# A fused attention and FFN kernel on one core: last denominators by a broadcast-sum matmul, b2 and b1 as matmul rows, and another table of the work's split

## The chip, the core and the metric

The kernel runs on one core of a Trainium2 chip. The core has a matrix engine (TensorE, PE in the profile), VectorE (DVE), ScalarE (ACT), GpSimd (POOL) and SyncE (SP), which issues transfers. The metric is the device time of one execution, in microseconds; before the change it is 747.16 us, the median of three runs (747.12 to 747.19).

## The reference

The input is a sequence of 2048 rows of 512. It is normalised, and the normalised rows go through two branches whose results are added to the input: attention with 32 query heads of 16 and a single shared key and value head, and a feed-forward layer of width 1792 with biases.

```python
xn = _layernorm(x, axis=-1)
return x + _A_ref(xn, A_wq, A_wk, A_wv, A_wo) + _B_ref(xn, B_w1, B_b1, B_w2, B_b2)
...
scores = jnp.einsum("bhqd,bkd->bhqk", q, k) * (Dh ** -0.5)
p = _softmax(scores, axis=-1)
o = jnp.einsum("bhqk,bkd->bhqd", p, v) 
...
h = _gelu(jnp.einsum("bsd,df->bsf", x, w1) + b1) 
return jnp.einsum("bsf,fd->bsd", h, w2) + b2
```

The attention result goes through `wo`, and the GELU is the tanh form. Most of the work is the softmax: 32 heads x 2048 x 2048 exponentials, 134 million.

## The kernel before

**Tiles.** The sequence is cut into four blocks of 512 query columns, and the heads into eight groups of four. For each block and group (32 head groups in all) the 16 key tiles of 128 are gone through for the four heads, so there are 2048 score tiles of 128 keys x 512 queries. Three tiles make a unit, and 683 units make the main part. `scores(u)` forms three tiles with three matmuls that run side by side on 32 rows of the array each (L968), into one half of six PSUM banks; the halves alternate.

**Who exponentiates what.** Each tile is done by one of two engines. ScalarE takes it with its exponential (`exp`, L991): two tiles of a unit in one instruction of 1024 columns, or three in one of 1536. Or VectorE takes it: one `tensor_scalar` adds a constant to the scores and writes them as int16 (L1022, `p1`), which are then read as bf16; the exponential's error is evened out by adding four shifted copies of the same tile. The shifts are made in batches of up to six tiles by three steps (`close_batch`): two on VectorE on the whole batch and on two copies at once (L1069), and one per tile that goes to GpSimd if it is free at that moment and to VectorE otherwise (L1065). A tile of ScalarE needs one matmul with V on PE, a tile of VectorE five (L1035). These use one of four column groups of 32, one for each head, and add up in bank 6. V carries a column of ones, so row 16 of each head's 32 rows is the softmax denominator. The string `DTAB` says for each unit which of its tiles VectorE takes; it is a constant of the file.

**Order.** Nothing is ordered by hand beyond that. All operations are recorded with their dependencies, a planner (`Prog.schedule`) goes through them with its own costs and puts each engine's instructions into one fixed order, and semaphores are placed. Side work (the products of the FFN, the query projections, the output projection) is placed behind units given by tables: `HP` for the first FFN product of each tile, `YP` for the output tiles, `QK` and `Q3` for queries. Fillers (matmuls with zeros) are put where the planner sees PE idle.

**FFN and GELU.** The first FFN product of a tile of 128 features x 512 rows (`h_mm`, four products of four column groups each, L674) goes into bank 7, and VectorE adds b1 from `b1T` and writes bf16 (L1177). The GELU is not taken there: it needs another table of ScalarE, so all GELUs are collected in two blocks, after units 182 and 512 (`GU`, function `gelu`). A block loads the table, and takes for two query blocks: seven tiles from SBUF in one instruction, three single tiles from PSUM, seven from SBUF, three from PSUM, five from SBUF, three from PSUM. The tiles from PSUM (`h_late`) were never evacuated by VectorE: their products stand in three banks of one half, ScalarE reads them with b1 as a bias operand (L1202), and the bank that it frees takes the product of the tile three places later. During a block the scores use one half of the banks, and VectorE takes all of the exponentials of the four or five units concerned. The table for the exponential is loaded again by the compiler ahead of the next exponential.

**Output.** When a head group ends, its 128 x 512 sums are copied to SBUF (`o_evac`, L1081). The denominators go by DMA into a dense form, are inverted by VectorE, go to memory and come back broadcast over 16 rows each, and GpSimd or VectorE multiplies (L1112) into `oTp`, two head groups to 128 rows. The output projection of a row tile (`wo_mm`) adds four such products, `y_mm` the second FFN product, `b2_mm` the bias as a product of ones and a row, all into bank 7.

**The tail.** The last head group takes no transfers. `o_norm_last` copies its sums in two halves (L1120), picks the denominators out with fp32 matmuls that bring them to 128 rows x 4 (`selL`, L668), inverts these on VectorE (L1126), spreads each over 32 columns (half of it on VectorE, L1132, half on ScalarE, L1134), transposes back on PE (L1137) and multiplies from PSUM (L1141). Then come the last projection (`wol`), three additions on VectorE (L1356), one copy on ScalarE (L1359) and four stores. The second-last head group shares no 128 rows with it: its 64 rows of `oTp` have zeros beneath them.

Of the kernel before, what the change touches and what calls it, by code (L numbers as in the profile page):

```python
# [60 lines left out]
DTAB = "o2t00o20.20.t0t.2.o2oot..0t0oo.o.2o2t2o220.200.t00tt.2.0o222o.002.020ttt0..t202ot.2.22222o.o002.t200o.0t..2002t22.2o.o2220t.t2o.2ooo02to..20t0o000.0.to00o0ot.2.22t2.0t0oo.0oo02t..020bXxxto0o0.tt220tot00.ot020t.t0tt..200t02t.t02o.2o202.2222t202.ot0000.2o.2.t0t2t0t0t2.00222o2o..t.2t02.22t02o.t2200o..222.o0.t.000o02o2.2o..ttoo.o.too0oo0.0t.22.2t22o.o0oo..2ot0.ooo.totot.22tt20o..2toto.02ott0t0.tt02oo.o00..to00to0t0..00t2o..t22o0to2002o.2tt2.022t.2.0ot00o0020o0t.20.ooo.t..00o0..t2o2o22o..t20.ootot0t0t02220t00.0bbXXB2t2o20t2.2o202t..t02t0..o2o2oo22t20o..200to20ot022..tt02t0.2.22o202t20too..202oot.ot20000ot0..2oto0.0t.2ot02o2020t.ot.022o2o..000o0t.to2o.2t0.0o.to2t0t0.o0.oto2.2t.o.."  # L61
# [14 lines left out]
HP = ((46.3963,25.57262,48.16392,137.89013,14,52.2867,77,21.34724,36.94639,135.1619,35.25214,143.76585,89,72.22155),(112.2259,74.41715,95,121.29838,157.97442,0,0,0,0,0,0,0,0,0),(328.87654,322.51607,297.61552,309.7649,294.71218,291.30051,286,332.83416,338.02598,344.7955,303.57085,313.20872,350.63119,488.80201),(479.44121,503.08827,457.33229,508.56788,448.62794,0,0,0,0,0,0,0,0,0))  # L76
YP = ((186.87977,183,230.37357,220.85148),(347,407.00376,373.24541,414.87978),(521,545,576.59107,557),(600,612.80493,650.61865,662))
# [460 lines left out]
def bass_parallel_sum__grouped_kv_mqa__dense_activation_gelu__prompt_kernel(  # L538
# [33 lines left out]
    with ExitStack() as es:  # L572
# [20 lines left out]
        b1row = sb([FT, P], bf, "b1row")  # L593
# [9 lines left out]
        selL = sb([P, 4], f32, "selL")  # L603
        rT = sb([P, 4, 4], f32, "rT")
# [32 lines left out]
        rX = rbP[:, 0, :].rearrange("p (i r) -> p i r", i=4)  # L637
# [54 lines left out]
        dma("sp", b1row[:], B_b1.rearrange("(k p) -> k p", p=P), "d_b1", w=["b1row"], due=0.6, lat=9.0)  # L692
# [43 lines left out]
        for gl in range(2):  # L736
# [3 lines left out]
        tload = act(lambda e: e.add_instruction(mybir.InstLoadActFuncSet(name=nc.get_next_instruction_name(), engine=e.engine,  # L740
                                                                         ins=[], outs=[], act_func_set_id=LNEXP_SET)),
# [337 lines left out]
        def o_evac(gg):  # L1079
# [23 lines left out]
            if end:  # L1103
                dve(lambda e: e.memset(oTp[64:P, sl, :], 0.0), r=[("Of", i)], w=[("oTp", sl)], n=200, lock=True)
# [300 lines left out]
```

## Time and profile before

| | |
|---|---|
| median of three runs | 747.16 us |
| the profiled execution, its own time | 747.11 us |
| its span, first to last instruction | 745.3 us |
| busy: PE, DVE, ACT, POOL | 729.3, 730.7, 730.1, 380.7 us |
| exponentials on ACT (L991) | 678 instructions, 676.9 us busy |
| score reads on DVE (L1022) | 552 instructions, 374.9 us busy |
| first GELU block | 209.26 to 225.56 us |
| second GELU block | 551.73 to 568.03 us |
| granted clock of TensorE | 1.000 |

The page gives busy time for each engine, a chain of work followed back from the last instruction, and groups of instructions by line with the mean duration of one. Instructions of one engine overlap a little, so that a mean duration is longer than the distance between two starts. PE's matmuls are pipelined, and its busy share says little of how near it is to its peak. The 1.81 us between the span and the execution's own time lie around the instructions.

### The profile page before, as it was taken

What the parts mean: (1) busy time and instruction counts of PE and PEld (TensorE: products, weight loads), DVE (VectorE), ACT (ScalarE), POOL (GpSimd) and SP (SyncE); (2) the same over time, 40 slices, a digit from 0 to 9 for tenths busy, and PEclk for the clock granted to TensorE, in tenths of its full rate; (3) what the DMA queues carried; (4) which work ended last, traced back from release to release, by engine and by line L of the source; (5) the groups of instructions that cost most, each with busy time, mean ns of one, the idle gap of its engine ahead of it and who ended that gap; (6) DMA issues with size and microseconds to landing.
All of it is one profiled execution on the core that took longest, in us unless ns stands there. A gap on an engine that the chain in (4) does not pass through costs nothing.

```text
span 745.3 us, 21947 instructions
## 1 busy us (share of the span) xinstructions
PE 729.3 (98%) x9050; PEld 222.9 (30%) x9050; DVE 730.7 (98%) x1402; ACT 730.1 (98%) x760; POOL 380.7 (51%) x528
## 2 busy tenths in 40 slices
PE   7999999999999999999999999999999999999998
PEld 5332322222232332223222222222233222322223
DVE  7899999999999999999999999999999999999996
ACT  8999999999999999999999999999999999999995
POOL 5445453566635465544636555454444555456361
PEclk9999999999999999999999999999999999999999
DMA  9200100101010010000101010100100001010010
GB/s 310 68 16 16 25 16 14 28 9 19 9 43 18 17 44 18 23 25 13 35 5 28 25 38 17 30 22 15 26 13 23 22 20 45 17 36 27 11 35 32
DMA packets 32076, 23.33 MB, mean 31 GB/s; under 512 B 16369, under 2 KB 27498, under 8 KB 31978
## 3 DMA queue, kind: packets, MB, share of 16 engines
q1 hardware_dynamic: 30922, 21.90, 11.0%
q8 instruction: 72, 1.18, 0.7%
q14 instruction: 26, 0.21, 0.1%
q10 hardware_dynamic: 1056, 0.03, 0.1%
HBM read 13.08 MB, written 2.35 MB: 21 GB/s over the span
## 4 chain that ended last, share of the span: by engine, by line
ACT 75%; PE 21%; DVE 3%; DMA 1%; issue 0%; SPq 0%
ACT E L991 70%; PE pAll L1035 10%; PE pAll L968 7%; PE pAll L674 4%; ACT ub L1198 2%; ACT x_sb L1202 1%; DVE Dt L1022 1%; PE pAll L668 1%; DVE stats L761 1%; ACT x_sb L1198 1%; DMA x_sb<-in_A_x_dram 1%; DVE Dt L1069 0%; ACT L991 0%; ACT L1198 0%; PE pAll L812 0%; ACT xnT L817 0%
## 5 line engine op out<-in xcount | busy, mean ns | idle before, releaser
L991 ACT ACTIVATE E<-pAll 128x1024 bf16<-128x1024 f32 (+1 forms) x678 | 676.9, 1242 | 2.1 <-PE pAll L968 2.0
L1065 POOL TENSOR_SCALAR Dt<-Dt 128x512 int16<-128x512 int16 x444 | 340.3, 766 | 326.8 <-DVE Dt L1069 136.3
L1035 PE MATMUL pAll<-Dt,V 128*32 128x512 bf16 x2825 | 422.4, 383 | 0.2
L1022 DVE TENSOR_SCALAR Dt<-pAll 128x512 int16<-128x512 f32 (+1 forms) x552 | 374.9, 693 | 2.8 <-PE pAll L968 2.1
L1069 DVE TENSOR_SCALAR Dt<-Dt 128x1024 int16<-128x1024 int16 (+6 forms) x518 | 290.8, 585 | 0.2
L968 PE MATMUL pAll<-QT,KT 32*128 32x512 bf16 x2048 | 267.2, 385 | 6.6 <-ACT E L991 4.1
L1035 PE MATMUL pAll<-E,V 128*32 128x512 bf16 x1483 | 272.1, 384 | 0.1
L968 PEld LDWEIGHTS pAll<-QT,KT 32*128 32x128 bf16 x2048 | 66.6, 91 | 288.4 <-ACT E L991 274.0
L1035 PEld LDWEIGHTS pAll<-Dt,V 128*32 128x32 bf16 x2825 | 108.8, 94 | 115.3 <-issue 76.8
L674 PE MATMUL pAll<-xnT,w_sb 128*32 128x512 bf16 x896 | 111.3, 382 | 0.9 <-ACT x_sb L1202 0.9
L1035 PEld LDWEIGHTS pAll<-E,V 128*32 128x32 bf16 x1483 | 64.6, 94 | 47.1 <-issue 31.9
L674 PE MATMUL pAll<-w_sb,ub 128*32 128x512 bf16 x448 | 70.0, 383 | 0.0
L674 PE MATMUL pAll<-w_sb,x_sb 128*32 128x512 bf16 x448 | 69.2, 383 | 0.0
L674 PE MATMUL pAll<-wop,oTp 128*32 128x512 bf16 x256 | 46.1, 383 | 0.0
L674 PEld LDWEIGHTS pAll<-xnT,w_sb 128*32 128x32 bf16 x896 | 31.2, 95 | 22.6 <-issue 9.5
L1065 DVE TENSOR_SCALAR Dt<-Dt 128x512 int16<-128x512 int16 x121 | 32.0, 282 | 0.0
L1112 POOL TENSOR_TENSOR oTp<-OfP,rbP 128x256 bf16<-128x256 f32 (+1 forms) x29 | 23.9, 831 | 13.7 <-DVE Dt L1069 9.2
L674 PE MATMUL pAll<-xnT,wq_sb 128*32 128x512 bf16 x256 | 24.3, 384 | 0.0
L1081 DVE COPY Of<-pAll 128x512 f32<-128x512 f32 x31 | 21.0, 679 | 0.0
L1177 DVE TENSOR_SCALAR ub<-pAll,b1T 128x512 bf16<-128x512 f32 x28 | 20.7, 739 | 0.0
L674 PEld LDWEIGHTS pAll<-w_sb,ub 128*32 128x32 bf16 x448 | 17.4, 94 | 5.5 <-issue 3.4
L674 PEld LDWEIGHTS pAll<-w_sb,x_sb 128*32 128x32 bf16 x448 | 16.6, 95 | 6.9 <-issue 5.2
(123 smaller groups left out, 251.7 us busy)
## 6 DMA issues: line engine op xcount, KB each, us to landing
OfP<-Of SPq DMA_DIRECT2D x124, 32.0 KB, 1.9
rbP<-rden_rows SPq DMA_DIRECT2D x124, 32.0 KB, 1.8
w_sb<-in_B_w_dram SPq DMA_DIRECT2D x2, 1792.0 KB, 12.7
x_sb<-in_A_x_dram SPq DMA_DIRECT2D x8, 256.0 KB, 4.6
x_sb<-in_A_x_dram SPq DMA_DIRECT2D x16, 128.0 KB, 2.1
QT<-qp SPq DMA_DIRECT2D x124, 16.0 KB, 1.8
out_dram<-x_sb SPq DMA_DIRECT2D x12, 128.0 KB, 1.7
wq_sb<-in_A_wq_dram SPq DMA_DIRECT2D x1, 512.0 KB, 6.4
```

Source lines behind the costliest of these rows:

```text
L668: return add("pe", lambda e: e.matmul(o, l, rh, start=start, stop=stop, **kw), r, w, occ=occ, lat=dlat[1], allow=allow, **ak)
L674: add("pe", lambda e, c=c, j=j: e.matmul(o[c, :], l[:, c], rh, start=start, stop=stop, tile_position=(0, 32 * j)), r, [(k, j) for k in w] ...
L968: ins = e.matmul(o, l, rh, start=True, stop=True, tile_position=(q0, 0))
L991: o = act(lambda e: e.activation(E[:, s0:s0 + na, :], bank(b0, na).rearrange("p (a n) -> p a n", a=na), ACT.Exp, scale=LN2 / 128.0), w=[B( ...
L1022: op = dve(lambda e: e.tensor_scalar(Dt[:, s:s + n, :], bank(bk, n).rearrange("p (a n) -> p a n", a=n), float(127 * 128) + SPL_D, SPL_MIN, ...
L1035: add("pe", lambda e, a, b: e.matmul(pO[32 * j:32 * j + 32, :], V1[:, v, kt, :], rhs, start=a, stop=b, tile_position=(0, 32 * j)), r=r + [ ...
L1065: add("pool", lambda e, d=d, k=k: e.tensor_scalar(d, d, 1.0, float(k), ALU.mult, ALU.add), [], [(("D", base[o > 0] + q), o)], occ=PL_OCC, ...
L1069: dve(lambda e, d=view(o, nb), q=view(i, nb), k=k: e.tensor_scalar(d, q, float(k), None, ALU.add), r=keys(i), w=keys(o), n=nb * n * TBW, m ...
L1081: dve(lambda e: e.tensor_copy(Of[:, i, :], pO), w=["O", ("Of", i)], allow=0.0)
L1112: "pool", lambda e, c=c: e.tensor_tensor(oTp[0:n, sl, c], OfP[0:n, s, c], rbP[0:n, s, c], ALU.mult),
L1177: dve(lambda e: e.tensor_scalar(ubs[tb % 2][:, ft, :], pM, b1T[:, ft:ft + 1], None, ALU.add), r=["b1T"], w=M4 + [ukey(tb, ft)], n=TBW + 57 ...
L1198: o = act(lambda e, uu=uu: e.activation(uu, uu, ACT.Gelu_apprx_tanh), r=uk, w=uk, n=len(uk) * TBW + 1200 * load + 50, kind="gelu", due=0.0 ...
```

## The change

Four things change, and with them the constants of the plan.

1. **Last denominators.** `selL` (128 x 4) becomes `selB` (128 x 128), in which every column of a head's 32 has a one at that head's denominator row. One fp32 matmul for each half of 256 columns gives the denominators already spread over the rows. ScalarE takes the logarithm of that from PSUM and then the exponential of its negative, in place of VectorE's reciprocal; the copies and transposes go. VectorE multiplies from SBUF.
2. **Last b2.** The 64 unused rows of `oTp` in the second-last group are set to 1 instead of 0, and their output weights are a new tile `wopE`, with 64 rows of `wo`, b2 in row 64, and zeros. For the last four row tiles `b2_mm` goes.
3. **FFN bias of the PSUM tiles as a matmul row.** `h_late` starts with a product of `b1row` (now 128 rows, zero past the 14) and one column of the identity, broadcast over 512 columns. ScalarE then needs no bias, and the first three PSUM tiles of each block are taken by one instruction of 1536 columns. The load of the table for the exponential is issued right behind the last GELU, and names the same set as the load at the start of the kernel. b1's transfer moves from the start of the kernel to behind the setup of K.
4. **The table.** `DTAB`, `HP`, `YP` have other values. Counted from the string, VectorE takes 568 tiles instead of 565.

In the order that results, ACT has 546 exponentials of two tiles and 128 of three (543 and 131 before), PE 72 bias matmuls more, 16 b2 matmuls less and 20 fillers more, POOL 453 of the one-tile steps (444 before).

The new constants of the plan (`DTAB`, `HP`, `YP`) are left out here.

```diff
-GU = tuple((u, tbs, n, (("s", tbs[0], 0, 7), ("p", tbs[1], 5), ("p", tbs[1], 6), ("p", tbs[1], 7), ("s", tbs[0], 7, 7), ("p", tbs[1], 8),
-                         ("p", tbs[1], 9), ("p", tbs[1], 10), ("s", tbs[1], 0, 5), ("p", tbs[1], 11), ("p", tbs[1], 12), ("p", tbs[1], 13)))
+GU = tuple((u, tbs, n, (("s", tbs[0], 0, 7), ("p", tbs[1], 5, 3), ("s", tbs[0], 7, 7), ("p", tbs[1], 8, 1), ("p", tbs[1], 9, 1),
+                         ("p", tbs[1], 10, 1), ("s", tbs[1], 0, 5), ("p", tbs[1], 11, 1), ("p", tbs[1], 12, 1), ("p", tbs[1], 13, 1)))
            for u, tbs, n in ((182, (0, 1), 5), (512, (2, 3), 5)))
+G_LOAD = (1.588, 1.405)
...
-        setup(lambda e: e.tensor_copy(selL[:], ident[:, 16:113:32]), r=["ident"], w=["selL"], due=24.0, after=late)
+        setup(lambda e: e.tensor_copy(selB[:].rearrange("p (j r) -> p j r", j=4), ident[:, 16:113:32].unsqueeze(2).to_broadcast([P, 4, 32])),
+              r=["ident"], w=["selB"], occ=0.3, due=24.0, after=late)
+        setup(lambda e: e.memset(wopE[:], 0.0), w=["wopE"], occ=0.4, due=24.0, after=late)
+        dma("sp", wopE[0:64, :], A_wo[(H - 2 * HG) * Dh:(H - HG) * Dh, :], "d_we", w=["wopE"])
+        dma("sp", wopE[64:65, :], B_b2.rearrange("(o n) -> o n", o=1), "d_we", w=["wopE"])
+        setup(lambda e: e.memset(b1row[:], 0.0), w=["b1row"], occ=0.16, due=24.0, after=late)
+        dma("sp", b1row[0:FT, :], B_b1.rearrange("(k p) -> k p", p=P), "d_b1", w=["b1row"])
...
-                dve(lambda e: e.memset(oTp[64:P, sl, :], 0.0), r=[("Of", i)], w=[("oTp", sl)], n=200, lock=True)
+                dve(lambda e: e.memset(oTp[64:P, sl, :], 1.0), r=[("Of", i)], w=[("oTp", sl)], n=200, lock=True)
...
         def o_norm_last(gg):
-            RB1 = [[("rbP", 0, h, j) for j in range(HG)] for h in range(2)]
             for h in range(2):
                 c = slice(h * 256, h * 256 + 256)
                 dve(lambda e, c=c: e.tensor_copy(Of[:, 1, c], pO[:, c]), w=["O", ("Of", 1), ("Of", 2 + h)], n=256, due=0.0)
             for h in range(2):
-                for i in (2 * h, 2 * h + 1):
-                    mm(bank(h)[:, 4 * i:4 * i + 4], Of[:, 1, i * P:(i + 1) * P], selL[:], True, True,
-                       r=[("Of", 2 + h), "selL"], w=[B(h)], occ=0.2, due=0.0)
-            for h in range(2):
-                dve(lambda e, h=h: e.reciprocal(rT[:, 2 * h:2 * h + 2, :],
-                                                bank(h)[:, 8 * h:8 * h + 8].rearrange("p (i j) -> p i j", j=4)),
-                    w=[B(h), ("rT", h)], n=100, due=0.0)
-                o = rX[:, 2 * h:2 * h + 2, :].rearrange("p i (j r) -> p i j r", j=4)
-                i_ = rT[:, 2 * h:2 * h + 2, :].unsqueeze(3).to_broadcast([P, 2, 4, 32])
-                if h == 0:
-                    dve(lambda e, o=o, i_=i_: e.tensor_copy(o, i_), r=[("rT", h)], w=[("rX", h)] + RB1[h], n=256, due=0.0)
-                else:
-                    act(lambda e, o=o, i_=i_: e.activation(o, i_, ACT.Copy), r=[("rT", h)], w=[("rX", h)] + RB1[h], n=256, due=0.0)
-            for h in range(2):
-                for i in (2 * h, 2 * h + 1):
-                    add("pe", lambda e, i=i, h=h: e.transpose(bank(h)[:, 128 + (i % 2) * P:256 + (i % 2) * P], rX[:, i, :], ident_f[:]),
-                        r=[("rX", h), "ident_f"], w=[B(h)], occ=0.15, lat=0.22, due=0.0)
+                c = slice(h * 256, h * 256 + 256)
+                mm(bank(h)[:, 0:256], selB[:], Of[:, 1, c], True, True, r=[("Of", 2 + h), "selB"], w=[B(h)], occ=0.44, due=0.0)
+            RB = [("rbP", 0, h, j) for h in range(2) for j in range(HG)]
             for h in range(2):
                 c = slice(h * 256, h * 256 + 256)
-                dve(lambda e, h=h, c=c: e.tensor_tensor(oT[:, c], Of[:, 1, c], bank(h)[:, 128:384], ALU.mult),
-                    r=[("Of", 2 + h)], w=[B(h), ("oTl", 0) if h == 0 else ("oTl", 1)], n=256, due=0.0)
+                act(lambda e, h=h, c=c: e.activation(rbP[:, 0, c], bank(h)[:, 0:256], ACT.Ln), w=[B(h), ("rbl", h)] + RB, n=256, due=0.0)
+            for h in range(2):
+                c = slice(h * 256, h * 256 + 256)
+                act(lambda e, c=c: e.activation(rbP[:, 0, c], rbP[:, 0, c], ACT.Exp, scale=-1.0), w=[("rbl", h)], n=256, due=0.0)
+            for h in range(2):
+                c = slice(h * 256, h * 256 + 256)
+                dve(lambda e, c=c: e.tensor_tensor(oT[:, c], Of[:, 1, c], rbP[:, 0, c], ALU.mult),
+                    r=[("Of", 2 + h), ("rbl", h)], w=[("oTl", h)], n=256, due=0.0)
...
         def h_late(tb, ft, bk):
+            mm4(bank(bk), b1row, ident[:, ft:ft + 1].to_broadcast([P, TBW]), True, False, r=["b1row", "ident"], w=[B(bk)], allow=HL_ALLOW)
             for d in range(DT):
-                mm4(bank(bk), w1_sb[:, d, ft * P:(ft + 1) * P], xnT[:, d, tb * TBW:(tb + 1) * TBW], d == 0, d == DT - 1,
+                mm4(bank(bk), w1_sb[:, d, ft * P:(ft + 1) * P], xnT[:, d, tb * TBW:(tb + 1) * TBW], False, d == DT - 1,
...
-                    o = act(lambda e, bk=bk, tb=tb, f0=f0: e.activation(ubs[tb % 2][:, f0, :], bank(bk), ACT.Gelu_apprx_tanh, bias=b1T[:, f0:f0 + 1]),
+                    o = act(lambda e, uu=uu, src=bank(3 * half[u] + b0, k).rearrange("p (a n) -> p a n", a=k): e.activation(uu, src, ACT.Gelu_apprx_tanh),
...
+            run = o.fn
+
+            def last(e):
+                ins = run(e)
+                e.add_instruction(act_set())
+                return ins
+            o.fn = last
...
         def y_tile(tb, i):
             y_mm(tb, i, al=YT_ALLOW[i])
-            wo_mm(tb, i, range(FIN_G), al=YT_ALLOW[i])
-            b2_mm(stop=i < 3, al=YT_ALLOW[i])
+            wo_mm(tb, i, range(FIN_G), al=YT_ALLOW[i], stop=i < 3)
```

Before the fused GELU of three tiles its three banks have to be full at once, and it frees them at once; in the order, the three bias products of the next three tiles come first, and the products of the three tiles alternate behind them.

More of the change, by code (lines that the diff above doesn't have):

```diff
@@ L1195, in gelu @@
                 if kind == "s":
-                    uu = ubs[tb % 2][:, f0:f0 + k[0], :]
-                    uk = [ukey(tb, f) for f in range(f0, f0 + k[0])]
-                    o = act(lambda e, uu=uu: e.activation(uu, uu, ACT.Gelu_apprx_tanh), r=uk, w=uk, n=len(uk) * TBW + 1200 * load + 50,
-                            kind="gelu", due=0.0, after=hold)
-                else:
-                    bk = 3 * half[u] + m % 3
-                    o = act(lambda e, bk=bk, tb=tb, f0=f0: e.activation(ubs[tb % 2][:, f0, :], bank(bk), ACT.Gelu_apprx_tanh, bias=b1T[:, f0:f0 + 1]),
-                            r=["b1T"], w=[B(bk), ukey(tb, f0)], n=TBW + 1200 * load, kind="gelu", due=0.0, after=hold)
-                    m += 1
-                    if m + 2 < len(late):
-                        h_late(*late[m + 2][1:], bk)
@@ L1207, in gelu @@
-                hold = [o]
+                    o = act(lambda e, uu=uu: e.activation(uu, uu, ACT.Gelu_apprx_tanh), r=uk, w=uk, n=nn, kind="gelu", due=0.0, after=hold)
+                else:
+                    b0 = m % 3
+                    assert b0 + k <= 3
+                    o = act(lambda e, uu=uu, src=bank(3 * half[u] + b0, k).rearrange("p (a n) -> p a n", a=k): e.activation(uu, src, ACT.Gelu_apprx_tanh),
+                            w=[B(3 * half[u] + b0 + i) for i in range(k)] + uk, n=nn, kind="gelu", due=0.0, after=hold)
+                    for i in range(m + 3, min(m + 3 + k, len(late))):
+                        h_late(*late[i], 3 * half[u] + i % 3)
+                    m += k
```

42 lines of the change are left out of this document (22 added, 20 removed).

## The prediction

> **What bounds the kernel now.** I read the page's busy line and its chain first, then busy time by stretch, then ScalarE's and VectorE's groups by shape, and last the two GELU blocks and the tail in order of time.
>
> ```profile
> PE 729.3 (98%) x9050; PEld 222.9 (30%) x9050; DVE 730.7 (98%) x1402; ACT 730.1 (98%) x760; POOL 380.7 (51%) x528
> ...
> ACT 75%; PE 21%; DVE 3%; DMA 1%; issue 0%; SPq 0%
> ```
>
> Three engines look full, but the chain of work that ended last runs through ScalarE (ACT) for 75% of the span and through VectorE (DVE) for 3%. The stretch between the two GELU blocks shows how much room each engine has:
>
> ```profile
> 225.56:551.73 326.17, 323.43 (x4008) 93.55 (x4004) 324.76 (x635) 326.13 (x328) 165.83 (x221) 1.00 0.09 23
> ```
>
> Columns after the length are PE, weight load, DVE, ACT, POOL, then the granted clock (1.00). ACT is idle for 0.04 us of 326 and DVE for 1.4. So time is the sum of ACT's and DVE's work, shared tile by tile: a saving on one engine counts in full only while the other keeps up. What follows the last exponential is a serial tail.
>
> ```profile
> ACT E L991 <- PE pAll L968: 2.0, 4, 0.5
> DVE Dt L1022 <- PE pAll L968: 2.1, 5, 0.8
> ```
>
> These are the waits of both engines for scores, 4.1 us in all. They are what another table can win back.
>
> **ScalarE: three tiles less.** Counted in the instruction order, the exponentials go from 543 pairs and 131 triples to 546 and 128: 1483 tiles become 1480.
>
> ```profile
> L991 ACT ACTIVATE E<-pAll 128x1024 bf16<-128x1024 f32 x543 | 527.7, 1163 | 2.1 <-PE pAll L968 2.0
> L991 ACT ACTIVATE E<-pAll 128x1536 bf16<-128x1536 f32 x131 | 203.8, 1587 | 0.0
> L1202 ACT ACTIVATE x_sb<-pAll,b1T 128x512 bf16<-128x512 f32 x18 | 11.1, 701 | 0.0
> L991 ACT ACTIVATE E<-pAll 128x512 bf16<-128x512 f32 x4 | 2.7, 686 | 0.0
> L1359 ACT ACTIVATE ub<-pAll 128x512 bf16<-128x512 f32 x1 | 0.6, 597 | 3.7 <-PE pAll L674 3.7
> ```
>
> 512 more columns cost 1587 - 1163 = 424 ns, so three tiles are 1.27 us less.
>
> **ScalarE: the GELU blocks.** The first one, from table load to table load:
>
> ```profile
> 209.26 1.28 ACT L1198 ACT_TABLE_LOAD   x1
> 210.56 3.19 ACT L1198 ACTIVATE ub<-ub 128x3584 bf16<-128x3584 bf16 x1
> 213.66 1.82 ACT L1202 ACTIVATE x_sb<-pAll,b1T 128x512 bf16<-128x512 f32 x3
> 215.36 3.19 ACT L1198 ACTIVATE ub<-ub 128x3584 bf16<-128x3584 bf16 x1
> 218.44 1.85 ACT L1202 ACTIVATE x_sb<-pAll,b1T 128x512 bf16<-128x512 f32 x3
> 220.15 2.37 ACT L1198 ACTIVATE x_sb<-x_sb 128x2560 bf16<-128x2560 bf16 x1
> 222.38 1.87 ACT L1202 ACTIVATE x_sb<-pAll,b1T 128x512 bf16<-128x512 f32 x3
> 224.27 1.28 ACT L991 ACT_TABLE_LOAD   x1
> ```
>
> From start to start the three groups of singles take 1.70, 1.71 and 1.89 us, 5.30 together, or 0.567 for a single. They lose the bias operand. The copy in L1359 has the same shape without one: 597 against 701 ns, 0.104 less. A single is then 0.463, three are 1.39, and the fused triple is 0.463 + 2 x 0.424 = 1.31. With the 0.18 that stands before the last load the groups come to 4.27: 1.03 us less a block, 2.06 for two. The other end is the 512-wide exponential, 686 ns, also without a bias: then the operand is worth 0.015, a block gains 0.41 and both 0.8. I take 2.06, since those four exponentials may have waited for scores. The Trainium skill, "ScalarE: Activation LUTs", section What ACT_TABLE_LOAD costs, gives about 93 ns for each pointer operand; as an estimate 18 of them are 1.67 us, where the two rows make it 1.87 or 0.27, so it sides with the copy.
>
> The load for the exponential is now issued right behind the last GELU. It gains nothing: in the rows above it already starts where the GELU ends, and the number of loads stays at five. The new Ln adds none.
>
> **What the blocks may give back.** The fused triple frees its three banks at once, not one each 0.57 us, and each bank now needs 5 x 4 matmuls (a bias row, then four products) where it needed 16. The order shows 60 matmuls in the second group with, in the first block, a score visit among them.
>
> ```profile
> 219.19 1.69 PE L674 MATMUL pAll<-xnT,w_sb 128*32 128x512 bf16 x27 [0.30 <-ACT x_sb L1202]
> ```
>
> Less the 0.38 of the last one, 27 matmuls are 6.75 rounds of four at 0.228 us. 15 rounds are 3.4 us, with 0.30 from release to first matmul and 0.15 until the last has ended 3.85. The SBUF GELU that covers this runs 3.1 us. ACT then waits 0.75 us a block, 1.5 for both. The bounds are nothing (if the bank that is needed first is filled first; but the three bias rows lead and the products interleave) and 1.1 a block with the score visit. PE is the only engine that this loads: 72 bias matmuls are 18 rounds or 4 us, 16 b2 matmuls go, 12 more value matmuls and 20 fillers come. Outside the blocks the waits for scores above bound what that can cost.
>
> ACT in sum: -1.27 - 2.06 + 1.5 = -1.8 us, from -3.3 to +0.1.
>
> **VectorE.** It takes the three tiles.
>
> ```profile
> L1022 DVE TENSOR_SCALAR Dt<-pAll 128x512 int16<-128x512 f32 x543 | 362.1, 680 | 2.8 <-PE pAll L968 2.1
> L1069 DVE TENSOR_SCALAR Dt<-Dt 128x2048 int16<-128x2048 int16 x90 | 61.1, 681 | 0.0
> L1069 DVE TENSOR_SCALAR Dt<-Dt 128x3072 int16<-128x3072 int16 x49 | 46.6, 952 | 0.0
> L1065 DVE TENSOR_SCALAR Dt<-Dt 128x512 int16<-128x512 int16 x121 | 32.0, 282 | 0.0
> L1069 DVE TENSOR_SCALAR Dt<-Dt 128x4096 int16<-128x4096 int16 x22 | 26.6, 1214 | 0.0
> L1069 DVE TENSOR_SCALAR Dt<-Dt 128x5120 int16<-128x5120 int16 x14 | 20.7, 1481 | 0.0
> L1069 DVE TENSOR_SCALAR Dt<-Dt 128x2560 int16<-128x2560 int16 x14 | 11.4, 814 | 0.0
> L1069 DVE TENSOR_SCALAR Dt<-Dt 128x6144 int16<-128x6144 int16 x6 | 10.5, 1748 | 0.0
> L1022 DVE TENSOR_SCALAR Dt<-pAll 128x1536 int16<-128x1536 f32 x4 | 7.0, 1744 | 0.0
> L1022 DVE TENSOR_SCALAR Dt<-pAll 128x1024 int16<-128x1024 f32 x5 | 6.0, 1211 | 0.0
> ...
> 734.29 0.68 DVE L1065 TENSOR_SCALAR Dt<-Dt 128x512 int16<-128x512 int16 x3
> ```
>
> Reads of scores: two more of 512, one less of 1024, one more of 1536: 1.36 - 1.21 + 1.74 = +1.89. Sums: eight more of 2048 and of 4096, one less of 2560 and of 5120, four less of 3072 and of 6144: 15.16 - 2.30 - 10.80 = +2.06. Six steps of L1065 leave DVE: -1.69. Together +2.27; neighbours overlap by 0.08 (three steps of 282 ns take 0.68 us in the last row, from the order of time), and two instructions more make it +2.1. Its ends are +1.9 and +2.3. GpSimd takes nine steps more, at 0.77 us; with 51% busy that is free, unless a step is late for its batch.
>
> **Start.** SP issues two more transfers and the b1 row moves behind the start of the main part; POOL gets two memsets and a larger copy.
>
> ```profile
> 28.41 3.13 SPq L681 DMA_DIRECT2D QT<-qp  x4
> 40.35 0.15 DVE L1259 COPY b1T<-pAll 128x14 f32<-128x14 f32 x1
> ```
>
> Ahead of the Q rows, which take 0.78 us an issue, now stand three more, some 2.3 us. The rows serve the second head group, 21 score triples into the kernel; at 326.17 us for 328 ACT instructions that is some 20 us after the first scores, over 10 us of slack. b1 is wanted at 40.35 and issued beside the Q rows: again some 10 us. The memsets delay the first steps of POOL, which is idle for 49% of the span. I cost all of it at nothing, and at 0.5 us if that cover goes.
>
> **Tail.**
>
> ```profile
> 724.52 11.62 ACT L991 ACTIVATE E<-pAll 128x1024 bf16<-128x1024 f32 x11
> 736.65 0.88 DVE L1120 COPY Of<-pAll 128x256 f32<-128x256 f32 x2 [1.68 <-PE pAll L1035]
> 737.16 1.05 PE L668 MATMUL pAll<-selL,Of 128*128 128x4 f32 x8
> 738.50 0.42 ACT L1134 ACTIVATE rbP<-rT 128x256 f32<-128x256 f32 x1 [2.36 <-DVE rT L1126]
> 738.91 0.44 PE L1137 MATMUL pAll<-ident_f,rbP 128*128 128x128 f32 x2
> 739.38 0.42 DVE L1141 TENSOR_TENSOR oT<-Of,pAll 128x256 bf16<-128x256 f32 x1 [0.92 <-PE pAll L1137]
> 740.08 0.42 DVE L1141 TENSOR_TENSOR oT<-Of,pAll 128x256 bf16<-128x256 f32 x1 [0.28 <-PE pAll L1137]
> 742.57 0.60 ACT L1359 ACTIVATE ub<-pAll 128x512 bf16<-128x512 f32 x1 [3.65 <-PE pAll L674]
> ```
>
> Now: first product at 737.16, 256 fp32 columns. Two transposes, also 256 columns, took 0.44, which is the lower end; a product may need more than a transpose, so I take 0.6 to its end and 0.45 to the start of the next, and double that as the upper end. Ln 0 starts near 737.8 and takes 0.42 as L1134 does; the second product ends at 738.2, Ln 1 runs 738.25 to 738.67, Exp 0 738.5 to 738.93, Exp 1 738.78 to 739.2. The two multiplications run 738.95 to 739.8. The second ended at 740.50, so 0.7 us less; behind it the order leaves 26 side matmuls and the last four, about as many as before. I take -0.6, from -1.0 to +0.3 if each fp32 product takes double. The Trainium skill, "FP8 and Floating Point Precision", section TensorE Precision Notes, has a true fp32 product go through the array in four passes; as an estimate from the 0.228 us of a bf16 round of 512 columns that is 0.46 and the end, 0.6; by it the sum stays, and by the transposes the tail is 0.15 shorter.
>
> **Sum.** The profiled execution took 747.11 us, 1.81 more than its span, and the median of the runs, 747.16, is 0.05 above it. ACT ends its exponentials at 736.14 (724.52 + 11.62), DVE its steps at 734.97 (734.29 + 0.68), on average 735.55. With -1.8 and +2.1 shared between them the average is 735.7; if both end together, that is 0.45 earlier than 736.14. Of the 4.1 us of waits I take half as won back by the new table, 1.0 for each engine (from 0 to 2). Main part -1.45, tail -0.6: span 743.25, median 745.1 us.
>
> **Rivals.** (1) ACT keeps the lead, no bank is late, and DVE's idle time takes its 2.1 us: -3.3 - 0.6 gives 743.3. For it: the chain's 75% on ACT. Against: DVE's 1.4 us of room in 326. (2) The parts cancel and the table wins nothing back: -0.45 - 0.6 gives 746.1. For it: the -1.8 and +2.1 themselves. (3) DVE becomes the engine that sets the end: its last step moves from 734.97 to 737.07, and with the 1.68 us that now lie before the copy of L1120 the tail starts 2.1 later: 747.16 + 2.1 - 0.6 = 748.7, slower. It leaves the kernel slower than before as long as the table wins back under 1.5 us of DVE's own idle time. For it: DVE gains work while ACT loses it. Against: half of that 1.68 us was a wait for ACT's last tile.
>
> **How the numbers follow.** About 0.2% (1.5 us) is what can be told from no change. Forecast 0.42, of it 0.39 under 745.66 and 0.03 above; rival 1 0.18, rival 2 0.22, rival 3 0.18, of it 0.16 beyond 748.6. Faster 0.57, same 0.27, slower 0.16. The range takes in rival 1 with the tail's lower end and some idle time, 742.4, and rival 3, 748.7; the forecast's own is 743.8 to 746.0.
>
> **What would show it.** GELU blocks of about 16.0 us (15.3 if no bank is late, with no idle time ahead of the second group); ACT's last exponential near 734.7 and DVE's last step within 1 us of it; waits for scores near 1 us on each engine; 3.2 us from the first copy of the last output to the end of the second multiplication, where 3.85 were. A DVE that ends over 1 us behind ACT, or an ACT waiting over 1 us in a block, makes it wrong.

## The result, and the profile after

The kernel after takes 746.03 us (median of 22 runs, 745.64 to 746.7), the kernel before 747.08 us in the same sessions (22 runs, 746.72 to 747.28). The ratio is 0.9986, with a 95% interval of 0.9980 to 0.9993: 1.05 us faster, about half of the 2.06 that were forecast. Its profiled execution took 746.57 us, 0.54 above the median, with a span of 744.8 us; it is one of the slower of the 22, whose spans run from 743.9 to 745.0 with a median of 744.3.

The page of the kernel after, busy time and the chain that ended last:

```profile
PE 731.4 (98%) x9128; PEld 226.7 (30%) x9130; DVE 731.0 (98%) x1401; ACT 728.9 (98%) x759; POOL 389.3 (52%) x539
...
ACT 65%; PE 30%; DVE 3%; DMA 1%; issue 0%; SPq 0%; POOL 0%
```

ACT's share of the chain falls from 75 to 65%, PE's rises from 21 to 30%. What I call the main part runs from the start of the first exponential to the end of the last. One row of busy time by stretch covers it; first before, then after (columns: stretch and length, PE, weight load, DVE, ACT, POOL, clock).

```profile
24.50:736.14 711.64, 704.42 (x8791) 207.62 (x8789) 707.69 (x1337) 709.96 (x707) 368.11 (x480) 1.00 0.09 22
```
```profile
24.69:735.66 710.97, 707.23 (x8872) 211.90 (x8870) 708.72 (x1339) 707.73 (x703) 376.55 (x491) 1.00 0.09 22
```

The main part is 0.67 us shorter. ACT's idle time in it went from 1.7 to 3.2 us, DVE's from 4.0 to 2.3: ACT works less and waits more. The waits and the groups of after by shape say the same (mean ns of one behind the busy time):

```profile
ACT E L999 <- PE pAll L976: 2.7, 6, 0.5
DVE Dt L1030 <- PE pAll L976: 0.6, 2, 0.4
```
```profile
L999 ACT ACTIVATE E<-pAll 128x1024 bf16<-128x1024 f32 x546 | 524.5, 1136 | 2.0 <-PE pAll L976 1.7
L999 ACT ACTIVATE E<-pAll 128x1536 bf16<-128x1536 f32 x128 | 193.4, 1554 | 1.0 <-PE pAll L976 1.0
L1202 ACT ACTIVATE x_sb<-pAll 128x512 bf16<-128x512 f32 x12 | 6.3, 610 | 0.7 <-PE pAll L674 0.5
```

The recorded duration of one shape varies (an exponential of two tiles takes 1.02 us at 226.48 and 1.27 us at 734.87 in before), so a busy engine can still be waiting inside an instruction. So I took for each shape the 5th percentile of the distance from one start to the next on its engine as its own work, and all above it as waiting, as an estimate. By that ACT's own work in the main part falls from 698.7 to 695.2 us and its waiting grows from 11.7 to 14.7; DVE's work rises from 697.0 to 699.2, its waiting falls from 13.2 to 10.7. By stretch, cut at the table loads and 36 us behind the first load of a block:

| stretch | before: length, ACT waits, DVE waits | after |
|---|---|---|
| to block 1 | 184.77, 3.48, 3.11 | 185.27, 3.75, 3.44 |
| block 1, load to load | 15.00, 0.20, 0.05 | 14.73, 0.82, 0.18 |
| behind it | 21.00, 0.29, 1.63 | 21.27, 0.76, 0.22 |
| to block 2 | 306.46, 4.36, 4.73 | 305.97, 5.15, 4.29 |
| block 2, load to load | 15.00, 0.20, 0.05 | 14.31, 0.41, 0.22 |
| behind it | 21.00, 0, 0.95 | 21.69, 0.69, 0.09 |
| to the last exponential | 147.13, 3.15, 2.65 | 146.62, 3.14, 2.23 |

The GELU blocks of after, ACT in order of time (block 1 and what follows it, then block 2):

```profile
219.41 1.57 ACT L1202 ACTIVATE x_sb<-pAll 128x512 bf16<-128x512 f32 x3 [0.55 <-PE pAll L674]
...
224.69 1.28 ACT L1212 ACT_TABLE_LOAD   x1
225.99 2.56 ACT L999 ACTIVATE E<-pAll 128x512 bf16<-128x512 f32 x3
228.74 1.02 ACT L999 ACTIVATE E<-pAll 128x1024 bf16<-128x1024 f32 x1 [0.19 <-PE pAll L976]
```
```profile
557.66 3.18 ACT L1198 ACTIVATE ub<-ub 128x3584 bf16<-128x3584 bf16 x1
560.97 1.57 ACT L1202 ACTIVATE x_sb<-pAll 128x512 bf16<-128x512 f32 x3
566.25 1.28 ACT L1212 ACT_TABLE_LOAD   x1
567.54 2.64 ACT L999 ACTIVATE E<-pAll 128x512 bf16<-128x512 f32 x3
```

The blocks take 16.02 and 15.61 us instead of 16.30, and each refill makes ACT wait. What follows them is the important part. Busy time in the 36 us from a block's first table load, both blocks, before and after:

```profile
209.26:245.26 36.00, 34.59 (x507) 12.15 (x504) 35.14 (x63) 35.96 (x35) 17.51 (x23) 1.00 0.13 32
551.73:587.73 36.00, 35.01 (x503) 12.09 (x499) 35.58 (x55) 35.96 (x35) 17.22 (x22) 1.00 0.10 23
```
```profile
209.97:245.97 36.00, 35.98 (x520) 13.28 (x520) 35.97 (x63) 35.20 (x33) 12.64 (x19) 1.00 0.11 26
551.93:587.93 36.00, 34.93 (x510) 14.02 (x511) 36.00 (x65) 35.73 (x33) 14.85 (x20) 1.00 0.12 25
```

Before, ACT is without a gap there (35.96 of 36) and DVE is idle for 0.86 and 0.42 us. After, DVE is without a gap (35.97 and 36.00) and ACT is idle for 0.80 and 0.27. The roles have changed. How DVE can then hold ACT up shows in DVE and PE in order of time behind block 1 of after:

```profile
225.48 1.74 DVE L1077 TENSOR_SCALAR Dt<-Dt 128x6144 int16<-128x6144 int16 x1
```
```profile
227.28 1.09 PE L1043 MATMUL pAll<-Dt,V 128*32 128x512 bf16 x10
228.30 0.39 PE L976 MATMUL pAll<-QT,KT 32*128 32x512 bf16 x3
```

The shift step of a large batch ends at 227.22; ten V products that read it stand in PE's order ahead of the next scores (228.30), and ACT's exponential starts at 228.74, after a wait of 0.19 us in the records.

The tail of after, PE's two fp32 products (two records each), then DVE's and then ACT's rows:

```profile
736.75 1.16 PE L668 MATMUL pAll<-Of,selB 128*128 128x256 f32 x4
```
```profile
736.27 0.89 DVE L1127 COPY Of<-pAll 128x256 f32<-128x256 f32 x2 [1.43 <-PE pAll L1043]
738.73 0.76 DVE L1140 TENSOR_TENSOR oT<-Of,rbP 128x256 bf16<-128x256 f32 x2 [1.57 <-ACT rbP L1137]
```
```profile
737.49 0.90 ACT L1134 ACTIVATE rbP<-pAll 128x256 f32<-128x256 f32 x2 [1.83 <-PE pAll L668]
738.29 0.71 ACT L1137 ACTIVATE rbP<-rbP 128x256 f32<-128x256 f32 x2
741.64 0.60 ACT L1365 ACTIVATE ub<-pAll 128x512 bf16<-128x512 f32 x1 [2.64 <-PE pAll L674]
```

From the first copy to the end of the second multiplication 3.22 us pass, 3.85 before. From the last exponential's end to ACT's copy it is 5.98 us, 6.43 before. Yet from that end to the end of the span it is 9.17 us in both traces: in this execution the gain is lost at the stores. SP's four store issues, from the start of the first to the end of the last, before and then after:

```profile
741.22 2.30 SPq L681 DMA_DIRECT2D out_dram<-ub  x4
```
```profile
740.45 2.58 SPq L681 DMA_DIRECT2D out_dram<-ub  x4
```

They start 0.77 us earlier and end only 0.49 earlier, and with the earlier end of the main part (0.48) nothing is left of it.

### The profile page after: what moved, and what is told of

The parts are those of the page before. It is cut to its first block, busy times and chain, and to the rows that moved or that the text cites. A ratio compares the mean times of both kernels' runs of the same rounds, so it can differ in the third digit from the quotient of the medians.

```text
span 744.8 us, 22104 instructions
## 1 busy us (share of the span) xinstructions
PE 731.4 (98%) x9128; PEld 226.7 (30%) x9130; DVE 731.0 (98%) x1401; ACT 728.9 (98%) x759; POOL 389.3 (52%) x539
## 4 chain that ended last, share of the span: by engine, by line
ACT 65%; PE 30%; DVE 3%; DMA 1%; issue 0%; SPq 0%; POOL 0%
ACT E L999 64%; PE pAll L1043 13%; PE pAll L976 9%; PE pAll L674 7%; DVE Dt L1030 1%; DVE Dt L1077 1%; DMA x_sb<-in_A_x_dram 1%; PE pAll L668 0%; PE pAll L814 0%; DVE stats L763 0%; ACT xnT L819 0%; PE pAll L1372 0%; ACT ub L796 0%; DVE Dt L1073 0%; DVE QT L865 0%
## 5 line engine op out<-in xcount | busy, mean ns | idle before, releaser
L1073 POOL TENSOR_SCALAR Dt<-Dt 128x512 int16<-128x512 int16 x453 | 348.5, 769 | 318.8 <-DVE Dt L1077 143.6
L1043 PE MATMUL pAll<-Dt,V 128*32 128x512 bf16 x2840 | 414.3, 383 | 0.8 <-DVE Of L1089 0.8
L1077 DVE TENSOR_SCALAR Dt<-Dt 128x1024 int16<-128x1024 int16 (+5 forms) x524 | 292.6, 582 | 0.3
L1043 PE MATMUL pAll<-E,V 128*32 128x512 bf16 x1480 | 278.4, 384 | 0.0
L674 PE MATMUL pAll<-xnT,w_sb 128*32 128x512 bf16 x896 | 104.7, 382 | 0.0
L1043 PEld LDWEIGHTS pAll<-E,V 128*32 128x32 bf16 x1480 | 66.3, 94 | 49.7 <-issue 36.0
L674 PE MATMUL pAll<-w_sb,x_sb 128*32 128x512 bf16 x448 | 71.7, 383 | 0.0
L1073 DVE TENSOR_SCALAR Dt<-Dt 128x512 int16<-128x512 int16 x115 | 30.1, 281 | 0.0
L1120 POOL TENSOR_TENSOR oTp<-OfP,rbP 128x256 bf16<-128x256 f32 x29 | 23.2, 808 | 11.7 <-DVE Dt L1030 5.1
```

The costliest lines, as they stand in the source:

```text
L674: add("pe", lambda e, c=c, j=j: e.matmul(o[c, :], l[:, c], rh, start=start, stop=stop, tile_position=(0, 32 * j)), r, [(k, j) for k in w] ...
L1043: add("pe", lambda e, a, b: e.matmul(pO[32 * j:32 * j + 32, :], V1[:, v, kt, :], rhs, start=a, stop=b, tile_position=(0, 32 * j)), r=r + [ ...
L1073: add("pool", lambda e, d=d, k=k: e.tensor_scalar(d, d, 1.0, float(k), ALU.mult, ALU.add), [], [(("D", base[o > 0] + q), o)], occ=PL_OCC, ...
L1077: dve(lambda e, d=view(o, nb), q=view(i, nb), k=k: e.tensor_scalar(d, q, float(k), None, ALU.add), r=keys(i), w=keys(o), n=nb * n * TBW, m ...
L1120: "pool", lambda e, c=c: e.tensor_tensor(oTp[0:n, sl, c], OfP[0:n, s, c], rbP[0:n, s, c], ALU.mult),
```

## The experiments

Times are medians; before ran beside each of them. Every kernel is compared with after by its ratio to before (after: 0.9986).

### What an engine's work is worth: four kernels with more work

After and before with 96 exponentials of 5 columns more on ACT (every 7th unit), or 79 score reads of 6 columns more on DVE (every 7th read), all into a scratch tile. The order of the rest does not change.

```diff
+                if more:
+                    e.tensor_scalar(scrD[:, no // 7, :], bank(bk)[:, 0:6], float(127 * 128) + SPL_D, SPL_MIN, ALU.add, ALU.max)
...
+                if u % 7 == 3:
+                    e.activation(scrA[:, u // 7, :], bank(b0)[:, 0:5], ACT.Exp, scale=LN2 / 128.0)
```

> The changed kernel with 79 small extra reads of scores on VectorE (6 columns, into a scratch tile), one ahead of every seventh score read; nothing else moves. At an estimated 0.07 us each that is 5.5 us of work, spread evenly. If VectorE sets the pace of the main part, the time grows by nearly all of it, 5 us; if both engines share the bound, by 2 to 3; if ScalarE leads, by under 1.

> The changed kernel with 96 small extra exponentials on ScalarE (5 columns, into a scratch tile), one ahead of every seventh unit's; nothing else moves. At an estimated 0.055 us each that is 5.3 us of work. If ScalarE leads, the time grows by nearly all of it, 5 us; if both engines share the bound, by 2 to 3; if VectorE sets the pace, by under 1.

> The same 79 extra reads on VectorE in the kernel before. If ScalarE led there, as the chain says, under 1 us; if both share the bound, 2 to 3. Less than in the changed kernel, if the change moved the pace towards VectorE.

> The same 96 extra exponentials on ScalarE in the kernel before. If ScalarE led there, nearly all of it, 5 us; if both share the bound, 2 to 3. More than in the changed kernel, if the change moved the pace towards VectorE.

Start to start an added exponential takes 0.055 us and an added read 0.072: 5.4 and 5.7 us in all. With more on ACT, after went to 752.04 us (ratio 1.0068, 1.0056 to 1.0081) and before to 753.48 (1.0086, 1.0072 to 1.0099). With more on DVE, after went to 747.35 (1.0004, 0.9995 to 1.0013) and before to 747.39 (1.0005, 0.9996 to 1.0014). The main part of after with more reads, after with more exponentials, before with more reads, before with more exponentials:

```profile
24.43:736.76 712.33, 707.92 (x8872) 215.54 (x8870) 710.97 (x1418) 708.54 (x703) 378.39 (x491) 1.00 0.09 22
```
```profile
24.40:741.58 717.18, 711.05 (x8872) 209.42 (x8870) 712.54 (x1339) 714.06 (x799) 377.51 (x491) 1.00 0.09 22
```
```profile
24.27:736.48 712.21, 705.21 (x8791) 210.99 (x8789) 709.50 (x1416) 710.41 (x707) 369.85 (x480) 1.00 0.09 22
```
```profile
24.54:742.53 717.99, 708.64 (x8791) 205.91 (x8789) 711.62 (x1337) 716.34 (x803) 369.02 (x480) 1.00 0.09 22
```

Against 710.97 and 711.64, a microsecond on ACT costs 1.15 us in after and 1.18 in before; one on DVE costs 0.24 and 0.10 (0.23 and 0.05 by the medians). So at a fixed split of the tiles time is not shared between the two: ACT sets it, for work spread over the kernel, and DVE has room, less of it in after. The 1.3 us that the reads cost after by the medians lie between the two expectations (under 1, and 2 to 3); why a microsecond on ACT costs more than one is open.

### The refill, bank by bank

After, with the 60 refill matmuls of a block reordered so that the bank that is needed first is filled first.

```diff
+        for group in refills:
+            where = {id(op): n for n, op in enumerate(pr.ops)}
+            for n, op in zip(sorted(where[id(op)] for op in group), list(group)):
+                pr.ops[n] = op
```

> The changed kernel with one thing else: behind the fused GELU of each block the 60 matmuls that refill its three banks fill one bank after the other, where they alternated; nothing else moves on any engine. ScalarE's wait ahead of the second group (0.55 us in the first block, 0.2 in the second) should go, and the blocks take 15.4 us. If ScalarE leads, the time falls by all of it, 0.8 us under the changed kernel; if both engines share the bound, by 0.4; if VectorE sets the pace, by nothing.

746.12 us, ratio 0.9985 (0.9976 to 0.9994): nothing gained. ACT in order of time, block 1 of this kernel:

```profile
218.53 1.68 ACT L1203 ACTIVATE x_sb<-pAll 128x512 bf16<-128x512 f32 x3
...
225.25 0.60 ACT L999 ACTIVATE E<-pAll 128x512 bf16<-128x512 f32 x1
226.38 1.94 ACT L999 ACTIVATE E<-pAll 128x1024 bf16<-128x1024 f32 x2 [0.53 <-PE pAll L976]
```

The wait of 0.55 us ahead of the second group is gone, and 0.53 us stand behind the block instead. The main part is 710.97 us, as in after. So the stall, which the prediction made the main loss in the blocks, costs nothing by itself under this plan: what ACT saves in the block it waits behind it.

### The blocks' length: the bias back in after, out of before

After with `b1T` as bias operand of the 14 GELUs from PSUM again; and before with the bias operand of its 18 left out.

```diff
-... ACT.Gelu_apprx_tanh),
+... ACT.Gelu_apprx_tanh, bias=b1T[:, f0:f0 + 1]),
```
```diff
-e.activation(ubs[tb % 2][:, f0, :], bank(bk), ACT.Gelu_apprx_tanh, bias=b1T[:, f0:f0 + 1])
+e.activation(ubs[tb % 2][:, f0, :], bank(bk), ACT.Gelu_apprx_tanh)
```

> The kernel after, with b1T back as ScalarE's bias operand in the 14 GELUs from PSUM (b1 is then counted twice in these tiles). ScalarE's own work grows by about 14 x 0.09 = 1.3 us, all of it inside the two GELU blocks; nothing else changes. Theory A (around a block VectorE's steps run without a gap and set when the next scores come, so a shorter block is given back behind it): at most 0.3 us more, 745.9 to 746.4 us, with ScalarE's waits behind the blocks (0.70 and 0.60 us now) shorter by what the blocks are longer. Rival (ScalarE sets the end everywhere, as its slope of about 1.1 for work spread over the whole kernel suggests): 1.4 us more, 747.4 us.

> The kernel before, with the bias operand of the 18 GELUs from PSUM left out (b1 is not added in these tiles); nothing else changes, order and table are those of before. ScalarE's work in the two blocks falls by 18 x 0.092 = 1.66 us. In before VectorE stands idle for 1.63 and 0.95 us behind the blocks. Theory A (whether a shorter block counts is decided by VectorE's room behind it, which the table of before leaves and that of after doesn't): 1.3 to 1.7 us less, 745.4 to 745.8 us. Rival (a shorter block is given back under any table, because PE's scores come no earlier): at most 0.3 us less, 746.8 us.

After with the bias back: 746.33 us, ratio 0.9988 (0.9980 to 0.9997). The blocks are 0.54 and 0.55 us longer, the main part only 0.16. Before without it: 745.44 us, ratio 0.9979 (0.9970 to 0.9988), 1.49 us less than the 746.93 of before beside it. Main part of after with the bias back, then main part and the two stretches of 36 us of before without it:

```profile
24.50:735.63 711.13, 707.17 (x8872) 210.54 (x8870) 708.86 (x1339) 708.38 (x703) 376.45 (x491) 1.00 0.10 22
```
```profile
24.70:734.72 710.02, 704.66 (x8791) 208.63 (x8789) 707.30 (x1337) 708.34 (x707) 368.42 (x480) 1.00 0.09 22
...
209.48:245.48 36.00, 35.66 (x518) 12.67 (x515) 35.88 (x65) 35.96 (x36) 17.52 (x23) 1.00 0.15 32
551.13:587.13 36.00, 35.81 (x515) 12.95 (x507) 36.00 (x56) 35.96 (x36) 18.24 (x22) 1.00 0.09 23
```

The same kind of saving counts nearly in full under the plan of before (1.62 of 1.66 us in the trace) and 0.16 of 1.09 under that of after. Under the plan of before ACT stays without a gap (35.96) and DVE's idle time is used up (from 35.14 and 35.58 to 35.88 and 36.00 busy); under that of after there was none left. The bias row or the table alone in the plan of before was not run, so no run says which of the two takes DVE's room. Single for single, 0.569 us from start to start became 0.477: 0.092 us for the operand, where the Trainium skill, "ScalarE: Activation LUTs", section What ACT_TABLE_LOAD costs, has about 93 ns; the trace agrees.

### VectorE relieved at the blocks

After, with DVE's shift steps at half their columns for the batches that begin in a block's five units; and the same with the refill bank by bank.

```diff
-[list(Dt[:].ap[0]), [step, nb], [1, n * TBW]])
+[list(Dt[:].ap[0]), [step, nb], [1, n * TBW // (2 if batch[0][0] // 3 in HALF else 1)]])
```

> The kernel after, with VectorE's shift steps on whole batches at half their columns for the batches that begin in the five units of each GELU block (half of these shifted copies is left out, so the sums of those tiles are not right). VectorE loses some 2.3 us of work a block, the order stays. Theory A: ScalarE's waits behind the blocks go, 1.1 to 1.3 us in all: 744.7 to 745.0 us. The rival that PE's added matmuls set the pace there: no change, 746.0 us. The rival that VectorE's work counts evenly over the kernel, with the 0.24 us per us that the added reads cost: 4.7 x 0.24 = 1.1 us too, but then with ScalarE's waits behind the blocks still there.

> The same, with the 60 refill matmuls of each block bank by bank as well. Bank by bank alone gained nothing over the kernel after: the wait ahead of the second group of singles went and came back behind the block. Theory A: with VectorE relieved the 0.55 and 0.2 us of that wait now count too: 743.9 to 744.3 us, 0.7 less than the relief alone. If PE sets the pace: no change against the relief alone.

745.30 us, ratio 0.9975 (0.9965 to 0.9985), and 745.02 us, 0.9971 (0.9960 to 0.9983). Main part and the two stretches of the first:

```profile
209.85:245.85 36.00, 35.98 (x528) 12.79 (x524) 34.70 (x64) 35.41 (x34) 13.03 (x20) 1.00 0.12 26
551.31:587.31 36.00, 35.12 (x514) 13.53 (x511) 35.10 (x66) 35.82 (x34) 14.65 (x21) 1.00 0.12 25
...
24.58:734.61 710.03, 706.48 (x8872) 210.18 (x8870) 705.66 (x1339) 707.10 (x703) 375.94 (x491) 1.00 0.10 23
```

By the medians that is 0.7 to 0.8 us under after, with intervals that overlap (after: 0.9980 to 0.9993). The main part of the traces is the finer measure: it is 711.64 to 711.66 us in before and the two kernels below that share its order up to the tail, and 710.97 in after, with the refill reordered and with the last store on another queue. Here it is 0.94 us shorter, and the waits behind the blocks account for it: 0.76 and 0.69 us became 0.33 and 0.23, where DVE work that counts evenly would have left them. PE's matmuls are as many as in after, so their number is not what held ACT up here. So DVE's work at the blocks is what makes ACT wait behind them; I had expected 1.1 to 1.3 us. With the refill as well the main part is 709.73 us, 0.30 less, where 0.7 was expected, and too little for the medians to tell: in block 2 the whole of the refill's 0.26 us counts now; in block 1, shorter by 0.51, it comes back as 0.46 of waiting. PE is without a gap there (35.97 of 36 us in this kernel, 34.59 before), so it may be the next in line; no run tests that.

### The tail alone, and the table loads

Before with the new tail and the explicit table load behind the last GELU; and the same without the explicit load, so that the compiler places it.

```diff
+                mm(bank(h)[:, 0:256], selB[:], Of[:, 1, c], True, True, r=[("Of", 2 + h), "selB"], w=[B(h)], occ=0.44, due=0.0)
...
+                e.add_instruction(act_set())
```

> The kernel before with the new tail alone (fp32 broadcast sum, Ln and Exp), and the load of the table for the exponential written out behind each GELU block, so that Ln and Exp find their set. The order of every engine up to the tail is that of the kernel before. If the tail is worth what the sum gave it, the time is 0.6 us under before and the second multiplication ends 3.2 us after the first copy starts. If what was won there is lost again at the stores, as the profile of the changed kernel suggests (one store took SP 1.02 us to issue), it is 0.1 to 0.2 us under before.

> As e1, but the loads of tables are left to the compiler, which puts one ahead of the first Ln and one ahead of the first Exp of the tail. If both loads lie on the path, 2 x 1.28 us more than e1, so 2.0 us over before. If the first one runs while ScalarE waits for the sums (it was idle for 1.8 us there), 1.3 us more than e1, 0.7 over before.

The tail alone: 746.60 us against 747.03, ratio 0.9994 (0.9986 to 1.0003); in the trace the main part is 711.66 us, and the tail behind it 8.50 instead of 9.17. The interval takes in no change. The medians show less than the trace because the time outside the span grew: 2.07 us in this kernel's runs (2.02 to 2.10) against 1.81 in before, for a reason that no run shows; within the span the median fell from 745.2 to 744.5 us. Without the explicit load 748.03 us, ratio 1.0013 (1.0005 to 1.0022), 1.43 us more. ACT in order of time, in the tail of that kernel:

```profile
735.99 1.28 ACT L1125 ACT_TABLE_LOAD   x1
737.73 0.87 ACT L1125 ACTIVATE rbP<-pAll 128x256 f32<-128x256 f32 x2 [0.46 <-PE pAll L666]
738.62 1.28 ACT L1128 ACT_TABLE_LOAD   x1
739.92 0.72 ACT L1128 ACTIVATE rbP<-rbP 128x256 f32<-128x256 f32 x2
```

The compiler puts a load ahead of Ln and one ahead of Exp. The first lies in ACT's wait, the second on the path. The prediction gave the moved load no value ("it gains nothing"); without it the new tail is a loss of 1.0 us (748.03 against 747.03).

### The last store on another queue

After, with the last store issued by ACT.

```diff
-            dma("sp", of[ti * P:(ti + 1) * P, :], ...
+            dma("act" if ti == NT - 1 else "sp", of[ti * P:(ti + 1) * P, :], ...
```

> The changed kernel with the last store issued by ScalarE, which makes its data, not by SP. If SP's slow issue of the store before it costs the tail 0.3 us, the time is 0.3 us under the changed kernel; if that was one execution's accident, it is the same.

746.09 us, ratio 0.9987 (0.9978 to 0.9996): no gain. In its trace the tail behind the main part takes 8.78 us, but an instruction fetch ended earlier there too, which the last part shows; by the medians the queue of the last store is not what the tail loses.

## Why the prediction was right or wrong

**The outcome.** Faster, as forecast, but 746.03 us where 745.1 stood, just above the forecast's own range (743.8 to 746.0). By the prediction's own line for no change (1.5 us, down to 745.66) the result counts as the same, though the interval excludes no change. That it lies in the whole range is in good part luck: 742.4 to 748.7 takes in every rival. The number is that of rival 2 (746.1), its reason is not: the parts did not cancel, a part was given back. The main part of the trace gained 0.67 us where 1.45 were forecast; of the 1.05 by the medians that leaves 0.4 for the rest, where 0.6 was forecast.

**ScalarE's work: right.** -1.27 and -2.06 were forecast, 3.3 us without the refill; measured were 3.5. The fused triple takes 1.33 us from start to start (1.31 forecast), a single 0.477 (0.463): the three groups of a block take 4.38 us (4.27). The refill stalls are 0.62 and 0.21 us, not 0.75 each (its round of 0.228 us follows from its row only if 27 matmuls count as 5.75 rounds; the refill's own rounds start 0.216 us apart): the distance from the second large GELU to the second group is 3.72 and 3.31 us where 3.1 had been. Block 1 came out at 16.02 (16.0), block 2 at 15.61.

**VectorE's work: right.** +2.1 forecast, +2.2 measured.

**The step that failed: "time is the sum of ACT's and DVE's work, shared tile by tile".** It failed twice. Over the whole kernel nothing is shared: the step takes half a microsecond for each on ACT or DVE, but ACT's work costs 1.15 to 1.18 us per us, DVE's 0.05 to 0.24. The row that it was read from shows both engines busy and could not tell: by the distances of starts, ACT waits some 4.6 us and DVE 6.4 in that stretch (0.29 + 4.36 and 1.63 + 4.73 in the table above). Rival 1 was right that ACT leads. And at the blocks it is the other way round, which an average over 326 us between them could not show: there DVE takes all exponentials of five units, and in after it has no room left behind them. A block of GELUs that is 0.9 us shorter in ACT's work then gives 0.62 and 0.21 to the refill and 0.47 and 0.71 to waits behind the block: 2.0 us in the two blocks, more than the 1.8 saved. Neither sign that would have made the prediction wrong came (DVE ended 0.82 us ahead of ACT, and ACT waited at most 0.82 us in a block): the signs looked into the block, and the loss lay behind it. The kernels with changed blocks show it: put back into after, the work costs almost nothing; taken out of before, it pays nearly in full; with DVE relieved, after gains. What is left of the main part's gain comes from outside the blocks: 1.7 us less work on ACT, the three tiles foremost, against 1.06 us more waiting there, and 0.17 because the last exponential itself takes 1.10 us instead of 1.27. Where those 1.06 us come from, the table, the added matmuls or DVE's denser work, no run takes apart.

**The table: half right.** Of the 4.1 us of waits for scores, 1.0 was to come back on each engine. DVE's fell from 2.1 to 0.6, ACT's rose from 2.0 to 2.7. It is ACT's that count.

**Start: right.** The first exponential starts between 24.27 and 24.70 us in all runs, with or without the change.

**Tail: mechanism right, end wrong.** 3.22 us for 3.2. The first fp32 product was done 0.70 us after its start and the second started 0.54 behind it, in part because its half of the sums was copied later; that is nearer to the estimate from four passes (0.6 and 0.46; the Trainium skill, "FP8 and Floating Point Precision", section TensorE Precision Notes) than to the transposes. ACT's last exponential ended at 735.66, not 734.7, DVE's last step 0.82 us before it. The -0.6 was reached within the span in the tail alone (0.67 in its trace; 0.43 by the medians, which hold the longer time outside the span) and vanished at the stores in the profiled execution of after: the sum ended at the multiplications and had no term for what the stores meet, nor for time outside the span.

**Rival 3**, DVE as the engine that sets the end, is refuted for the whole kernel by the added reads; as far as the runs show, DVE holds ACT up only in the 20 us or so behind each block.

## What to carry to other kernels

Read room where the saved time would have to be used: extend the stretch past the end of the saved work, and see which engine is without a gap there. If it is not the one that got faster, the saving comes back as a wait a few microseconds later, and removing one visible stall only moves it. Measure an engine's price by a few tiny extra instructions, before and after, rather than infer it from busy shares that are all 98%.

## What the runs showed of the hardware that was not expected

**A store's issue takes longer where an instruction fetch overlaps it.** Transfers of queue 8, kind instruction, move 16 KB in about 1 us; one stands close to the tail. The DMA view of after for 740 to 742 us (40 slices of 0.05 us, busy share in tenths; below it the queue's share of 16 engines):

```profile
DMA  0000000900000000000000000047999986320020
...
q8 instruction: 1, 0.02, 4.1%
```

It starts at 740.37 and takes 1.32 us; the first store is issued at 740.45, the second at 741.05, and that issue lasts 1.02 us instead of 0.36. Times behind the last exponential's end, in us, from the traces:

| kernel | fetch ends | second issue ends | end of the span |
|---|---|---|---|
| before | 1.33 | 6.04 | 9.17 |
| new tail in before | 1.34 | 5.66 | 8.50 |
| after, more exponentials | 5.46 | 5.84 | 8.67 |
| after, more reads | 5.57 | 5.93 | 8.80 |
| after | 6.04 | 6.41 | 9.17 |
| after, refill bank by bank | 6.04 | 6.41 | 9.16 |
| after, relieved | 6.19 | 6.57 | 9.30 |

In all kernels with the instructions of after the second issue ends 0.36 to 0.38 us behind the fetch (0.36 in the one with the last store on ACT, whose fetch ends at 5.63). SP's issues of two of them, after with more exponentials and after relieved:

```profile
746.31 2.14 SPq L682 DMA_DIRECT2D out_dram<-ub  x4
```
```profile
739.40 2.73 SPq L681 DMA_DIRECT2D out_dram<-ub  x4
```

In the kernels with the order of before the fetch starts 0.1 to 0.4 us behind the last exponential and ends over 3 us ahead of the stores, and in those of after 4.5 to 5.2 us behind it, among the stores; what places it no run shows. By the last column it may be worth up to 0.6 us among the kernels of after. It is a coincidence of times in every trace and was not tested by moving a fetch. The Trainium skill, "Runtime: NRT & Kernel Launch", section Instruction fetch mechanics, has each sequencer fetch blocks of 16 KiB by a DMA queue of its own, at a cost that is mostly hidden; the size agrees, and here the cost does not look hidden.

**Short instructions.** An exponential of 5 columns stands 0.32 us in the records and takes 0.055 us from start to start; a read of 6 columns 0.15 and 0.072. A mean duration says little of what an instruction adds.
